# Ordering the first three K/V projection tiles by weight chunk in a fused linear-attention and GLU kernel

## Chip, cores and metric

The kernel runs on one core of a Trainium2 chip. The metric is the device time of one execution in microseconds (us), as the median of several executions. One profiled execution of each kernel shows where the time goes; a profile's span is about 1.7 us shorter than the time of the same execution. The record marks an execution as slow when it lies over 1.5% above the fastest of its kernel. TensorE is called PE (its weight loads PEld), VectorE DVE, ScalarE ACT, GpSimd POOL.

## The reference

The input `x` is 2048 x 1024 in bf16. Only the first part matters here:

```python
qkv = layernorm(x) @ wqkv            # 1024 -> 3 x 1024, 32 heads of 32
phi = lambda t: where(t > 0, t + 1, exp(t)) + 1e-6
kv  = einsum("bhsd,bhse->bhde", phi(k), v)      # summed over all 2048 rows
z   = einsum("bhsd->bhd", phi(k))
o   = (phi(q) @ kv) / (phi(q) . z + 1e-6)
h   = x + o @ wo
# ... then h2 = h + gated MLP(layernorm(h)), well over half of the time
```

## The kernel before

The kernel first makes K and V for 16 row tiles of 128 rows and sums `kv` over them in PSUM, the memory that the matmuls write to. For each tile: layer norm on DVE (with one power on POOL), eight PE transposes (`pt`), a copy to `xnT` on ACT, 16 K matmuls and 16 V matmuls of 128x512 each, and eight small `kv_bank` matmuls. The weights for K and V come in four chunks of 1 MB: two for K (n = 0, 1), two for V.

```python
def ln_transpose(t):
    if t not in x_tiles: load_x(t)              # x tiles: a ring of 3 buffers
    ...                                         # statistics, rstd on POOL, xn on DVE
    for kc in range(KC): nc.tensor.transpose(pt[:, kc, :], xn[...], ident[:])
    nc.scalar.copy(out=xnT[:, :, t * P:(t + 1) * P], in_=pt[:])

def kv_tile(t):
    for n in range(NDC):                        # K: 2 chunks of 8 matmuls
        ...  k_ps += xnT[t] @ wkv_sb[n]
        phi_from_psum(...)                      # exp on ACT, two steps on DVE -> pk_t
    for n in range(NDC):                        # V: 2 chunks of 8 matmuls
        ...  v_ps += xnT[t] @ wkv_sb[NDC + n]
        nc.scalar.copy(out=v_aug[...], in_=v_ps[...])
    for c in range(KC): nc.tensor.matmul(kv_banks[...], lhsT=pk_t[...], rhs=v_aug[...])

for t in range(3): load_x(t)
for i in range(2 * NDC): load_wkv(i)            # 4 x 1 MB, each in 4 DMAs
ln_transpose(0)
for t in range(ST):
    if t + 1 < ST: ln_transpose(t + 1)
    kv_tile(t)
    if t == 1: nc.sync.dma_start(out=wo_sb[:], in_=wo_v)     # 2 MB, needed much later
# ... q projection, attention, MLP
```

A scheduler fixes the order of instructions on each engine when the kernel is built. Each engine then works through its own list in that order, so an instruction that waits holds up all those behind it (in wo_early below, V matmuls whose weights and `xnT` had long been there stood 6.25 us behind tile 3's transposes).

Of the kernel before, what the change touches and what calls it, by code (L numbers as in the profile page):

```python
# [10 lines left out]
FP32 = mybir.dt.float32  # L11
BF16 = mybir.dt.bfloat16
# [9 lines left out]
def kernel(  # L22
# [10 lines left out]
    n_heads: int = N_HEADS,  # L33
    s_half: int = 1024,
    att_banks: int = 2,
):
    nc = tc.nc
    P = nc.NUM_PARTITIONS
# [3 lines left out]
    S, D = x.shape  # L42
    H = n_heads
    Dh = D // H
# [3 lines left out]
    HPC = P // Dh  # L48
    KC = D // P
    ST = S // P  # L50
    FT = F // P
    DW = Dh + 1
# [5 lines left out]
    CW = min(512, D)  # L58
    assert D % CW == 0
    NDC = D // CW  # L60
    CPC = CW // P
# [12 lines left out]
    wo_v = A_wo.rearrange("(kc p) n -> p kc n", p=P)  # L74
# [10 lines left out]
        out=mask[:], in_=mask[:], compare_op=ALU.is_ge, fill=0.0, base=0,  # L85
# [3 lines left out]
        out=mask[:], in_=mask[:], compare_op=ALU.is_ge, fill=0.0, base=Dh - 1,  # L89
# [9 lines left out]
    wo_sb = consts.tile([P, KC, D], BF16)  # L99
# [6 lines left out]
    def ps_tile(shape, dtype, name, tag="bank"):  # L106
        return psum.tile(shape, dtype, tag=tag, name=name, bufs=ps_bufs[tag])

    def layer_norm_stats(pool, src, name):
        fmax = nc.vector.BN_STATS_FMAX  # L110
        nsub = (D + fmax - 1) // fmax
        assert D % nsub == 0
        sub = D // nsub
        st = pool.tile([P, nsub, nc.vector.BN_STATS_DIM], FP32, name=f"{name}_st")
        for i in range(nsub):
            nc.vector.bn_stats(out=st[:, i, :], in_=src[:, i * sub:(i + 1) * sub])  # L116
        mv = pool.tile([P, nc.vector.BN_AGGR_DIM], FP32, name=f"{name}_mv")
        nc.vector.bn_aggr(out=mv[:], in_=st[:])
        rstd = pool.tile([P, 1], FP32, name=f"{name}_rstd")
        nc.vector.tensor_scalar(out=rstd[:], in0=mv[:, 1:2], scalar1=LN_EPS, scalar2=None, op0=ALU.add)  # L120
        nc.gpsimd.tensor_tensor(out=rstd[:], in0=rstd[:], in1=neg_half[:], op=ALU.pow)  # L121
        return mv[:, 0:1], rstd[:, 0:1]

    def phi_from_psum(pool, src_ps, dst, width):
        e = pool.tile([P, width], FP32, name="phi_e")
        nc.scalar.activation(out=e[:], in_=src_ps, func=ACT.Exp)  # L126
        nc.vector.tensor_scalar(out=e[:], in0=e[:], scalar1=PHI_EPS, scalar2=1.0 + PHI_EPS,  # L127
                                op0=ALU.add, op1=ALU.min)
        nc.vector.scalar_tensor_tensor(out=dst, in0=src_ps, scalar=1.0 + PHI_EPS, in1=e[:],
                                       op0=ALU.add, op1=ALU.max)  # L130
# [8 lines left out]
    with ExitStack() as p1:  # L139
        wkvpool = p1.enter_context(tc.tile_pool(name="wkvpool", bufs=2 * NDC))  # L140
        xpool = p1.enter_context(tc.tile_pool(name="xpool", bufs=3))
        pkvpool = p1.enter_context(tc.tile_pool(name="pkvpool", bufs=3))
        small1 = p1.enter_context(tc.tile_pool(name="small1", bufs=4))
        tmp1 = p1.enter_context(tc.tile_pool(name="tmp1", bufs=3))
        wqpool = p1.enter_context(tc.tile_pool(name="wqpool", bufs=NDC))
        big1 = p1.enter_context(tc.tile_pool(name="big1", bufs=1))
        xnT = big1.tile([P, KC, S], BF16)

        assert NKVB <= 2 * att_banks - 1
        kv_banks = []  # L150
        for b in range(NKVB):
            kb = ps_tile([P, KV_PER_BANK, NW], FP32, f"kv_bank{b}", tag=("attA" if b < att_banks else "attB"))
            nc.vector.memset(kb[:], 0.0)
            kv_banks.append(kb)

        wkv_sb = []
        KSPLIT = 4 if KC % 4 == 0 else 1

        def load_wkv(i):
            w_sb = wkvpool.tile([P, KC, CW], BF16, name="wkv_sb")  # L160
            col = D + i * CW
            kg = KC // KSPLIT
            for j in range(KSPLIT):
                nc.sync.dma_start(out=w_sb[:, j * kg:(j + 1) * kg, :], in_=wq_v[:, j * kg:(j + 1) * kg, col:col + CW])
            wkv_sb.append(w_sb)

        x_tiles = {}

        def load_x(t):
            x_sb = xpool.tile([P, D], BF16, name="x_sb")  # L170
            nc.sync.dma_start(out=x_sb[:], in_=x[t * P:(t + 1) * P, :])
            x_tiles[t] = x_sb

        def ln_transpose(t):
            if t not in x_tiles:
                load_x(t)
            x_sb = x_tiles.pop(t)
            mean, rstd = layer_norm_stats(small1, x_sb, "ln1")
            xn = xpool.tile([P, D], BF16, name="xn")
            nc.vector.tensor_scalar(out=xn[:], in0=x_sb[:], scalar1=mean, scalar2=rstd,  # L180
                                    op0=ALU.subtract, op1=ALU.mult)
            pt = ps_tile([P, KC, P], BF16, "pt", tag="bank")
            for kc in range(KC):
                nc.tensor.transpose(pt[:, kc, :], xn[:, kc * P:(kc + 1) * P], ident[:])
            nc.scalar.copy(out=xnT[:, :, t * P:(t + 1) * P], in_=pt[:])  # L185

        def kv_tile(t):
            pk_t = pkvpool.tile([P, D], BF16, name="pk_t")
            for n in range(NDC):
                k_ps = ps_tile([P, CW], FP32, "k_ps")  # L190
                for kc in range(KC):
                    nc.tensor.matmul(k_ps[:], lhsT=xnT[:, kc, t * P:(t + 1) * P], rhs=wkv_sb[n][:, kc, :],  # L192
                                     start=(kc == 0), stop=(kc == KC - 1))
                phi_from_psum(tmp1, k_ps[:], pk_t[:, n * CW:(n + 1) * CW], CW)
            v_aug = pkvpool.tile([P, KC, HPC, DW], BF16, name="v_aug")
            nc.gpsimd.memset(v_aug[:, :, :, Dh:DW], 1.0)
            for n in range(NDC):
                v_ps = ps_tile([P, CW], FP32, "v_ps")
                for kc in range(KC):
                    nc.tensor.matmul(v_ps[:], lhsT=xnT[:, kc, t * P:(t + 1) * P], rhs=wkv_sb[NDC + n][:, kc, :],  # L200
                                     start=(kc == 0), stop=(kc == KC - 1))
                nc.scalar.copy(out=v_aug[:, n * CPC:(n + 1) * CPC, :, 0:Dh],  # L202
                               in_=v_ps[:].rearrange("p (c h e) -> p c h e", c=CPC, h=HPC))
            for c in range(KC):
                b, j = divmod(c, KV_PER_BANK)
                nc.tensor.matmul(kv_banks[b][:, j, :], lhsT=pk_t[:, c * P:(c + 1) * P],  # L206
                                 rhs=v_aug[:, c].rearrange("p h e -> p (h e)"),
                                 start=False, stop=(t == ST - 1), skip_group_check=True)

        for t in range(min(3, ST)):  # L210
            load_x(t)
        for i in range(2 * NDC):
            load_wkv(i)

        ln_transpose(0)
        for t in range(ST):
            if t + 1 < ST:
                ln_transpose(t + 1)
            kv_tile(t)
            if t == 1:  # L220
                nc.sync.dma_start(out=wo_sb[:], in_=wo_v)

        for c in range(KC):
            b, j = divmod(c, KV_PER_BANK)
            nc.vector.tensor_tensor(out=kvaug[:, c], in0=kv_banks[b][:, j, :].rearrange("p (h e) -> p h e", h=HPC),
                                    in1=mask[:], op=ALU.mult)

        wq_sb = []
        for n in range(NDC):
            w_sb = wqpool.tile([P, KC, CW], BF16, name="wq_sb")  # L230
            nc.sync.dma_start(out=w_sb[:], in_=wq_v[:, :, n * CW:(n + 1) * CW])
            wq_sb.append(w_sb)
        prio_before_q = tc.cur_priority
        tc.cur_priority += 100000
        for sc in range(NSC):
            for c in range(KC):
                n, cl = divmod(c, CPC)
                q_ps = ps_tile([P, SC], FP32, "q_ps")
                for kc in range(KC):
                    nc.tensor.matmul(q_ps[:], lhsT=wq_sb[n][:, kc, cl * P:(cl + 1) * P],  # L240
                                     rhs=xnT[:, kc, sc * SC:(sc + 1) * SC],
                                     start=(kc == 0), stop=(kc == KC - 1))
                pq_sb = tmp1.tile([P, SC], BF16, name="pq_sb")
                phi_from_psum(tmp1, q_ps[:], pq_sb[:], SC)
                nc.gpsimd.dma_start(out=pq_dram[sc][c, :, :], in_=pq_sb[:])
        prio_after_q = tc.cur_priority
# [172 lines left out]
```

## Time and profile before

| | before |
|---|---|
| time, median of 4 executions | 872.94 us (872.92 to 873.72) |
| span of the profiled execution | 872.0 us |
| PE busy | 845.0 us, 97% |
| first PE instruction / first K matmul | 8.60 / 10.74 us |
| tile 3's first K matmul | 37.20 us |

The page's busy line of the kernel before reads: busy us of each engine, share of the span, instructions.

```profile
PE 845.0 (97%) x4267; PEld 397.3 (46%) x4352; DVE 350.6 (40%) x715; ACT 191.7 (22%) x273; POOL 42.2 (5%) x92
```

PE is the limit. A change at the start can gain only by starting the chain of PE work earlier or by closing gaps in it. The PE timeline of the kernel before shows them. Columns: start, length (overlapping ends are modelled), engine, line, operation, output<-inputs, count, and in brackets the idle time just ahead and what ended it.

```profile
10.74 5.41 PE L192 MATMUL k_ps<-wkv_sb,xnT 128*128 128x512 bf16 x16 [0.25 <-ACT xnT L185]
...
24.02 3.62 PE L200 MATMUL v_ps<-wkv_sb,xnT 128*128 128x512 bf16 x16
27.48 0.40 PE L206 MATMUL kv_bank<-v_aug,pk_t 128*128 128x132 bf16 x4
28.48 0.29 PE L184 MATMUL pt<-ident,xn 128*128 128x128 bf16 x2 [0.60 <-DVE xn L180]
...
32.62 3.62 PE L200 MATMUL v_ps<-wkv_sb,xnT 128*128 128x512 bf16 x16
36.08 0.40 PE L206 MATMUL kv_bank<-v_aug,pk_t 128*128 128x132 bf16 x4
36.31 0.55 PE L184 MATMUL pt<-ident,xn 128*128 128x128 bf16 x7
36.91 0.40 PE L206 MATMUL kv_bank<-v_aug,pk_t 128*128 128x132 bf16 x4
37.15 0.22 PE L184 MATMUL pt<-ident,xn 128*128 128x128 bf16 x1
37.20 3.62 PE L192 MATMUL k_ps<-wkv_sb,xnT 128*128 128x512 bf16 x15
40.65 3.62 PE L200 MATMUL v_ps<-wkv_sb,xnT 128*128 128x512 bf16 x16
```

The reader is to see three things. The first K matmul is released by the ACT copy, not by a weight. There is one named stop, at 28.48 us: tile 3's transposes wait for the DVE's `xn`. And each turnover, the transposes and `kv_bank` matmuls between the V of one tile and the K of the next, takes 37.20 - 36.08 = 1.12 us.

The first 16 K matmuls take 5.25 us (10.74 to 15.99), later ones 3.45 us. The weight-load timeline of the kernel before (one load per matmul) shows why.

```profile
13.28 0.15 PEld L192 LDWEIGHTS <-xnT 128*128 128x128 bf16 x1 [0.28 <-issue]
13.70 0.15 PEld L192 LDWEIGHTS <-xnT 128*128 128x128 bf16 x1 [0.28 <-issue]
...
14.48 0.10 PEld L192 LDWEIGHTS <-xnT 128*128 128x128 bf16 x1 [0.20 <-issue]
```

The starts are an even 0.427 us apart and then drop to 0.216 us. The even spacing has "issue" and no DMA as what ended the idle time, and it ends where the trace's record has the clock full, at 14.39 us: these matmuls were slow by the clock. The Trainium skill, "TensorE: Matmul & The Clock Gate", "Wait — 56ns, not 53.3ns?", gives 426.7 and 215.7 ns for these two states, and this trace agrees.

The stop at 28.48 us comes from the DVE. Its timeline in the kernel before shows tile 3's statistics behind the first of tile 1's phi steps. The x tile itself was no earlier: its load, queued behind `wo`, landed at 24.25 us, 10.5 us after its issue.

```profile
23.59 0.69 DVE L129 SCALAR_TENSOR_TENSOR pk_t<-k_ps,phi_e 128x512 bf16<-128x512 f32 x1
24.27 0.69 DVE L116 BATCH_NORM_STATS2 ln_st<-x_sb 128x6 f32<-128x512 bf16 x1
...
27.87 0.55 DVE L180 TENSOR_SCALAR xn<-x_sb,ln_mv,ln_rstd 128x1024 bf16<-128x1024 bf16 x1
```

### The profile page before, as it was taken

What the parts mean: (1) busy time and instruction counts of PE and PEld (TensorE: products, weight loads), DVE (VectorE), ACT (ScalarE), POOL (GpSimd) and SP (SyncE); (2) the same over time, 40 slices, a digit from 0 to 9 for tenths busy, and PEclk for the clock granted to TensorE, in tenths of its full rate; (3) what the DMA queues carried; (4) which work ended last, traced back from release to release, by engine and by line L of the source; (5) the groups of instructions that cost most, each with busy time, mean ns of one, the idle gap of its engine ahead of it and who ended that gap; (6) DMA issues with size and microseconds to landing.
All of it is one profiled execution on the core that took longest, in us unless ns stands there. A gap on an engine that the chain in (4) does not pass through costs nothing.

```text
span 872.0 us, 10492 instructions
## 1 busy us (share of the span) xinstructions
PE 845.0 (97%) x4267; PEld 397.3 (46%) x4352; DVE 350.6 (40%) x715; ACT 191.7 (22%) x273; POOL 42.2 (5%) x92
## 2 busy tenths in 40 slices
PE   5999999999999999999999999999999999999998
PEld 3455554444444444444444444444444444444443
DVE  4854324778776414213312411632242142133124
ACT  3344443354534210110011011211101101100110
POOL 2111001211210000000000000000000000000000
PEclk9999999999999999999999999999999999999999
DMA  9710005432352032232232103332311322322002
GB/s 314 240 37 26 0 1 173 135 97 68 97 157 61 13 100 70 85 97 73 85 97 73 56 29 96 121 133 77 93 25 60 97 73 84 97 73 85 1 12 85
DMA packets 73185, 74.09 MB, mean 85 GB/s; under 512 B 18864, under 2 KB 57776, under 8 KB 73136
## 3 DMA queue, kind: packets, MB, share of 16 engines
q1 hardware_dynamic: 71600, 69.21, 25.5%
q0 software_dynamic: 1536, 4.20, 1.4%
q8 instruction: 34, 0.56, 0.3%
q14 instruction: 15, 0.12, 0.0%
HBM read 65.01 MB, written 8.39 MB: 84 GB/s over the span
## 4 chain that ended last, share of the span: by engine, by line
PE 86%; DVE 4%; ACT 3%; issue 2%; DMA 2%; POOL 1%; another core or an unknown queue 0%; SPq 0%; POOLq 0%; ACTq 0%; DVEq 0%
PE u_ps L347 22%; PE g_ps L342 21%; PE d_ps L366 20%; PE k_ps L192 6%; PE v_ps L200 6%; PE wo_ps L284 5%; PE q_ps L240 3%; ACT hn L293 1%; DVE ln_st L116 1%; DVE h_sb L286 1%; ACT v_aug L202 1%; DMA pq_dram<-pq_sb 1%; PE hnT_ps L296 1%; POOL ln_rstd L121 1%; PE kv_bank L206 1%
## 5 line engine op out<-in xcount | busy, mean ns | idle before, releaser
L342 PE MATMUL g_ps<-hnT,wg_sb 128*128 128x512 bf16 x878 | 212.1, 379 | 1.0
L347 PE MATMUL u_ps<-hnT,wu_sb 128*128 128x512 bf16 x878 | 210.8, 379 | 0.8
L352 DVE TENSOR_TENSOR hh<-u_ps,rg 128x512 bf16<-128x512 f32 x112 | 77.3, 690 | 296.2 <-PE u_ps L347 284.9
L366 PE MATMUL d_ps<-wd_sb,hh 128*128 128x512 bf16 x877 | 194.6, 379 | 1.0
L351 ACT ACTIVATE rg<-g_ps 128x512 f32<-128x512 f32 x112 | 66.9, 597 | 460.2 <-PE g_ps L342 454.5
L366 PEld LDWEIGHTS <-hh 128*128 128x128 bf16 x896 | 87.5, 98 | 104.3
L347 PEld LDWEIGHTS <-wu_sb 128*128 128x128 bf16 x896 | 87.3, 98 | 103.4
L342 PEld LDWEIGHTS <-wg_sb 128*128 128x128 bf16 x896 | 87.2, 98 | 102.9
L370 DVE TENSOR_TENSOR h_sb<-d_ps,h_sb 128x512 f32<-128x512 f32 x96 | 66.4, 692 | 78.2 <-PE d_ps L366 77.4
L284 PE MATMUL wo_ps<-wo_sb,oT_sb 128*128 128x512 bf16 x247 | 58.7, 380 | 1.1
L192 PE MATMUL k_ps<-wkv_sb,xnT 128*128 128x512 bf16 x248 | 59.1, 388 | 0.6 <-ACT xnT L185 0.3
L240 PE MATMUL q_ps<-xnT,wq_sb 128*128 128x512 bf16 x249 | 58.8, 379 | 0.2
L200 PE MATMUL v_ps<-wkv_sb,xnT 128*128 128x512 bf16 x250 | 57.5, 379 | 0.4
L127 DVE TENSOR_SCALAR phi_e<-phi_e 128x512 f32<-128x512 f32 x64 | 27.2, 425 | 57.7 <-ACT phi_e L126 57.4
L200 PEld LDWEIGHTS <-xnT 128*128 128x128 bf16 x256 | 25.1, 98 | 30.2
L284 PEld LDWEIGHTS <-oT_sb 128*128 128x128 bf16 x256 | 23.5, 98 | 32.8 <-ACT oT_sb L280 7.8
L192 PEld LDWEIGHTS <-xnT 128*128 128x128 bf16 x256 | 24.7, 99 | 28.1 <-issue 2.4
L121 POOL TENSOR_TENSOR ln_rstd<-ln_rstd,neg_half 128x1 f32<-128x1 f32 x32 | 18.1, 574 | 398.4 <-DVE ln_rstd L120 394.2
L240 PEld LDWEIGHTS <-wq_sb 128*128 128x128 bf16 x256 | 24.0, 98 | 24.0
L286 DVE TENSOR_TENSOR h_sb<-wo_ps,x_sb 128x512 f32<-128x512 f32 x32 | 21.9, 689 | 20.6 <-PE wo_ps L284 18.6
L370 DVE TENSOR_TENSOR o_out<-d_ps,h_sb 128x512 bf16<-128x512 f32 x32 | 21.9, 683 | 19.5 <-PE d_ps L366 18.7
L126 ACT ACTIVATE phi_e<-q_ps 128x512 f32<-128x512 f32 x32 | 19.1, 598 | 36.3 <-PE q_ps L240 32.9
(44 smaller groups left out, 391.5 us busy)
## 6 DMA issues: line engine op xcount, KB each, us to landing
wd_sb<-in_B_W_down_dram SPq DMA_DIRECT2D x8, 1792.0 KB, 8.4
x_sb<-in_A_x_dram SPq DMA_DIRECT2D x32, 256.0 KB, 2.8
wg_sb<-in_B_W_gate_dram SPq DMA_DIRECT2D x8, 1024.0 KB, 5.3
wu_sb<-in_B_W_up_dram SPq DMA_DIRECT2D x8, 1024.0 KB, 7.4
wg_sb<-in_B_W_gate_dram SPq DMA_DIRECT2D x8, 768.0 KB, 4.8
wu_sb<-in_B_W_up_dram SPq DMA_DIRECT2D x8, 768.0 KB, 6.5
wkv_sb<-in_A_wqkv_dram SPq DMA_DIRECT2D x16, 256.0 KB, 5.9
pq_dram<-pq_sb POOLq DMA_DIRECT2D x32, 128.0 KB, 2.4
```

Source lines behind the costliest of these rows:

```text
L127: nc.vector.tensor_scalar(out=e[:], in0=e[:], scalar1=PHI_EPS, scalar2=1.0 + PHI_EPS, op0=ALU.add, op1=ALU.min)
L192: nc.tensor.matmul(k_ps[:], lhsT=xnT[:, kc, t * P:(t + 1) * P], rhs=wkv_sb[n][:, kc, :], start=(kc == 0), stop=(kc == KC - 1))
L200: nc.tensor.matmul(v_ps[:], lhsT=xnT[:, kc, t * P:(t + 1) * P], rhs=wkv_sb[NDC + n][:, kc, :], start=(kc == 0), stop=(kc == KC - 1))
L240: nc.tensor.matmul(q_ps[:], lhsT=wq_sb[n][:, kc, cl * P:(cl + 1) * P], rhs=xnT[:, kc, sc * SC:(sc + 1) * SC], start=(kc == 0), stop=(kc == ...
L284: nc.tensor.matmul(wo_ps[:], lhsT=oT_sb[:, c, :], rhs=wo_sb[:, c, cc * CW:(cc + 1) * CW], start=(c == 0), stop=(c == KC - 1))
L286: nc.vector.tensor_tensor(out=h_sb[:, cc * CW:(cc + 1) * CW], in0=wo_ps[:], in1=x_sb[:, cc * CW:(cc + 1) * CW], op=ALU.add)
L342: nc.tensor.matmul(g_ps[:], lhsT=wg_sb[:, kc, ftl * P:(ftl + 1) * P], rhs=hnT_chunks[sc][:, kc, :], start=(kc == 0), stop=(kc == KC - 1))
L347: nc.tensor.matmul(u_ps[:], lhsT=wu_sb[:, kc, ftl * P:(ftl + 1) * P], rhs=hnT_chunks[sc][:, kc, :], start=(kc == 0), stop=(kc == KC - 1))
L351: nc.scalar.activation(out=rg[:], in_=g_ps[:], func=ACT.Relu)
L352: nc.vector.tensor_tensor(out=hh[:, sc * SC:(sc + 1) * SC], in0=u_ps[:], in1=rg[:], op=ALU.mult)
L366: nc.tensor.matmul(d_ps[:], lhsT=hh_tiles[j][:, stl * P:(stl + 1) * P], rhs=wd_sb[:, j, cc * CW:(cc + 1) * CW], start=(j == 0), stop=(j == ...
L370: nc.vector.tensor_tensor(out=dst[:, cc * CW:(cc + 1) * CW], in0=d_ps[:], in1=h_sb[:, cc * CW:(cc + 1) * CW], op=ALU.add)
```

## The change

Its intent: matmuls that use the first weight chunk can start while the others are still on their way. So the first three tiles all use K chunk 0, then all K chunk 1, and so on; `kv_bank` matmuls come at the end of the group. With it, tile 3's layer norm and transposes move into the middle of the group, and the load of x tile 3 goes out ahead of the 2 MB `wo` load instead of behind it.

```diff
@@ (cut: kv_tile is split into k_part(t, n), v_part(t, n), kv_part(t), bodies unchanged;
@@  pk_t and v_aug get pools of their own, three buffers each as before)
+        G = min(start_group, ST)          # start_group = 3
         ln_transpose(0)
-        for t in range(ST):
+        for n in range(NDC):
+            for t in range(G):
+                if n == 0 and t + 1 < G:
+                    ln_transpose(t + 1)
+                k_part(t, n)
+        if G < ST:
+            ln_transpose(G)
+        for n in range(NDC):
+            for t in range(G):
+                v_part(t, n)
+        for t in range(G):
+            kv_part(t)
+        nc.sync.dma_start(out=wo_sb[:], in_=wo_v)
+        for t in range(G, ST):
             if t + 1 < ST:
                 ln_transpose(t + 1)
             kv_tile(t)
-            if t == 1:
-                nc.sync.dma_start(out=wo_sb[:], in_=wo_v)
```

More of the change, by code (lines that the diff above doesn't have):

```diff
@@ L35 @@
     att_banks: int = 2,
+    start_group: int = 3,
 ):
@@ L141 @@
         xpool = p1.enter_context(tc.tile_pool(name="xpool", bufs=3))
-        pkvpool = p1.enter_context(tc.tile_pool(name="pkvpool", bufs=3))
+        pkvpool = p1.enter_context(tc.tile_pool(name="pkvpool", bufs=max(3, start_group)))
+        pkpool = p1.enter_context(tc.tile_pool(name="pkpool", bufs=max(3, start_group)))
         small1 = p1.enter_context(tc.tile_pool(name="small1", bufs=4))
@@ L185, in ln_transpose @@
             nc.scalar.copy(out=xnT[:, :, t * P:(t + 1) * P], in_=pt[:])
-        def kv_tile(t):
-            pk_t = pkvpool.tile([P, D], BF16, name="pk_t")
-            for n in range(NDC):
-                k_ps = ps_tile([P, CW], FP32, "k_ps")
-                for kc in range(KC):
-                    nc.tensor.matmul(k_ps[:], lhsT=xnT[:, kc, t * P:(t + 1) * P], rhs=wkv_sb[n][:, kc, :],
-                                     start=(kc == 0), stop=(kc == KC - 1))
-                phi_from_psum(tmp1, k_ps[:], pk_t[:, n * CW:(n + 1) * CW], CW)
-            v_aug = pkvpool.tile([P, KC, HPC, DW], BF16, name="v_aug")
-            nc.gpsimd.memset(v_aug[:, :, :, Dh:DW], 1.0)
-            for n in range(NDC):
-                v_ps = ps_tile([P, CW], FP32, "v_ps")
-                for kc in range(KC):
-                    nc.tensor.matmul(v_ps[:], lhsT=xnT[:, kc, t * P:(t + 1) * P], rhs=wkv_sb[NDC + n][:, kc, :],
-                                     start=(kc == 0), stop=(kc == KC - 1))
-                nc.scalar.copy(out=v_aug[:, n * CPC:(n + 1) * CPC, :, 0:Dh],
-                               in_=v_ps[:].rearrange("p (c h e) -> p c h e", c=CPC, h=HPC))
+        pk_tiles = {}
@@ new lines, with k_part @@
+        vaug_tiles = {}
+        def k_part(t, n):
+            if t not in pk_tiles:
+                pk_tiles[t] = pkpool.tile([P, D], BF16, name="pk_t")
+            pk_t = pk_tiles[t]
+            k_ps = ps_tile([P, CW], FP32, "k_ps")
+            for kc in range(KC):
+                nc.tensor.matmul(k_ps[:], lhsT=xnT[:, kc, t * P:(t + 1) * P], rhs=wkv_sb[n][:, kc, :],
+                                 start=(kc == 0), stop=(kc == KC - 1))
+            phi_from_psum(tmp1, k_ps[:], pk_t[:, n * CW:(n + 1) * CW], CW)
@@ new lines, in v_part @@
+        def v_part(t, n):
+            if t not in vaug_tiles:
+                v_aug = pkvpool.tile([P, KC, HPC, DW], BF16, name="v_aug")
+                nc.gpsimd.memset(v_aug[:, :, :, Dh:DW], 1.0)
+                vaug_tiles[t] = v_aug
+            v_aug = vaug_tiles[t]
+            v_ps = ps_tile([P, CW], FP32, "v_ps")
+            for kc in range(KC):
+                nc.tensor.matmul(v_ps[:], lhsT=xnT[:, kc, t * P:(t + 1) * P], rhs=wkv_sb[NDC + n][:, kc, :],
+                                 start=(kc == 0), stop=(kc == KC - 1))
+            nc.scalar.copy(out=v_aug[:, n * CPC:(n + 1) * CPC, :, 0:Dh],
+                           in_=v_ps[:].rearrange("p (c h e) -> p c h e", c=CPC, h=HPC))
@@ L204, in kv_tile, with kv_part @@
+        def kv_part(t):
+            pk_t = pk_tiles.pop(t)
+            v_aug = vaug_tiles.pop(t)
             for c in range(KC):
@@ L208, in kv_tile @@
                                  start=False, stop=(t == ST - 1), skip_group_check=True)
+        def kv_tile(t):
+            for n in range(NDC):
[3 more added lines that the diff above has]
+            kv_part(t)
         for t in range(min(3, ST)):
@@ L213 @@
             load_wkv(i)
+        G = min(start_group, ST)
         ln_transpose(0)
-        for t in range(ST):
+        for n in range(NDC):
+            for t in range(G):
+                if n == 0 and t + 1 < G:
+                    ln_transpose(t + 1)
+                k_part(t, n)
+        if G < ST:
+            ln_transpose(G)
+        for n in range(NDC):
+            for t in range(G):
+                v_part(t, n)
+        for t in range(G):
+            kv_part(t)
+        nc.sync.dma_start(out=wo_sb[:], in_=wo_v)
+        for t in range(G, ST):
             if t + 1 < ST:
```

## The prediction

> **What bounds the kernel now.** The page's busy table: TensorE (PE) is busy 845.0 of 872.0 us (97%); in the chain of waits PE holds 86%. The only large gap is the start: in the PE timeline the first instruction is at 8.60 us (x load, layer norm), the first K matmul at 10.74 us. From there to 140 us PE is nearly gapless.
>
> **Does the start wait for weights, as the change assumes?** No. The first K matmul's releaser is the ACT copy of xnT (0.25 us). The first eight K matmuls are slow (weight loads start 0.43 us apart until 14.1 us, 0.216 us afterwards), but evenly so: the cold clock. The Trainium skill, "TensorE: Matmul & The Clock Gate", "Wait — 56ns, not 53.3ns?", states 426.7 ns at N=512 cold and 215.7 ns warm, which agrees. So the 1.7 us lost there is not DMA. The weight chunks (16 DMAs issued from 2.2 to 12.5 us, median 5.9 us to landing) arrive just ahead of use: tile 0 runs from 14.1 to 19.6 us at full rate, and the waits view lists no PE wait on a weight DMA.
>
> **What the change moves.** The same 96 projection matmuls, 24 transposes and 24 kv matmuls, the same memory; after tile 3 the PE's instruction order is unchanged. New order: two tiles' transposes, 8 K, 8 transposes, 40 K, 8 transposes, 48 V, 24 kv, 8 transposes, then as before. The load of x tile 3 now goes ahead of the 2 MB wo load.
>
> **On the critical path.**
> - Before has one stall: layer norm of tile 3 is late (x tile 3 queued behind wo), PE idle 0.60 us at 28.5 us, released by DVE xn. V starts at 24.02, 32.62, 40.65: 8.60 against the steady 8.03. The earlier x load and the longer K run remove it: -0.57 us.
> - Each steady turnover loses 0.14 us: 8.03 against 32 x 0.216 + 8 x 0.060 + 8 x 0.064 = 7.90 (the last four kv matmuls wait for the 0.60 us ACT copy of v_aug). At the group's end the first 16 kv matmuls take 0.95 us and cover that copy: three turnovers, up to -0.42 us.
> - Extra switches between transposes and K: estimate +0.1 us.
> - New waits I looked for: K needs one PSUM bank per 1.73 us, and ACT 0.60 + DVE 1.12 us per bank keep up. DVE blocks on x tile 3 until about 19 us (estimate: issue 12.9 + 5.9), within four banks' slack.
>
> Sum: -0.9 us of 872.94, about 0.1%. PE is critical to the end, so it should survive as a rigid shift: 872.0 us, range 871.3 to 872.9. Chances: faster by 2% 0.01, within 2% 0.98, slower by 2% 0.01.
>
> **What would show each step.** First K matmul still near 10.74 us, first eight still 0.43 us apart, no weight-DMA wait in either kernel; the idle at 28.5 us gone; tile 3's K at about 36.4 us instead of 37.37; later PE pieces earlier by 0.9 us; PE busy time nearly unchanged.
>
> **What would make it wrong.** The cold clock ending at another moment (part of its 1.7 us either way). The DVE, now placed to normalise tiles 4 to 9 before tile 3's phi, blocking on x loads behind 4 MB of wo and wq, so that K finds no free bank (1 to 3 us lost). The attention stage absorbing the shift in a DMA wait (0.89 us at 162.6 us).

## The result

| | before | after |
|---|---|---|
| time, median | 872.94 us (872.26 to 873.72, 15 runs) | 871.57 us (871.11 to 874.64, 10 runs) |
| ratio | | 0.9987, 95% interval 0.9978 to 0.9996 |
| span of the profiled execution | 872.0 us | 870.2 us |
| first K matmul | 10.74 us | 10.57 us |
| tile 3's first K matmul | 37.20 us | 35.41 us |

A ratio is the mean time of one kernel's fast runs over that of the other's of the same rounds, so it is not quite the ratio of the medians. The medians differ by 1.37 us. The profiles differ more, 1.8 us, partly because the profiled execution of before was the slowest of its 15 (873.72 us).

The page's busy line of the kernel after, and its PE timeline to the point where tile 3 begins:

```profile
PE 844.1 (97%) x4267; PEld 397.3 (46%) x4352; DVE 350.4 (40%) x715; ACT 191.4 (22%) x273; POOL 42.2 (5%) x92
```

```profile
10.56 3.28 PE L198 MATMUL k_ps<-wkv_sb,xnT 128*128 128x512 bf16 x8 [0.25 <-ACT xnT L187]
13.68 0.61 PE L186 MATMUL pt<-ident,xn 128*128 128x128 bf16 x8
14.13 8.80 PE L198 MATMUL k_ps<-wkv_sb,xnT 128*128 128x512 bf16 x39
22.76 0.61 PE L186 MATMUL pt<-ident,xn 128*128 128x128 bf16 x8
23.21 10.52 PE L210 MATMUL v_ps<-wkv_sb,xnT 128*128 128x512 bf16 x47
33.57 1.56 PE L220 MATMUL kv_bank<-v_aug,pk_t 128*128 128x132 bf16 x24
34.97 0.61 PE L186 MATMUL pt<-ident,xn 128*128 128x128 bf16 x8
35.41 0.81 PE L198 MATMUL k_ps<-wkv_sb,xnT 128*128 128x512 bf16 x2
```

(A count of 39 or 47 is one record missing from the trace; the times show 40 and 48.) The first K matmul is no earlier for the change: it waits for the same ACT copy, and the 0.17 us come before it, from the x load and layer norm. The stop at 28.48 us is gone, and the three turnovers have become one.

From first K to tile 3's K it took 26.46 us before and 24.84 us after, 1.62 us less. The clock explains part: in this execution it was full at 13.39 us, in the profile of before at 14.39 us (the trace's record of the granted clock). I take the cold clock's cost as what the first K matmuls take over their 3.45 us for 16 (or 1.73 us for 8) at the full rate: 1.80 us before, 1.38 us after. What is left for the order of work is 1.62 - 0.42 = 1.20 us.

### The profile page after: what moved, and what is told of

Its sections match the earlier page's. It is cut to its first block, busy times and chain, and to the rows that moved or that the text cites. A ratio compares the mean times of both kernels' runs of the same rounds, so it can differ in the third digit from the quotient of the medians.

```text
span 870.2 us, 10491 instructions
## 1 busy us (share of the span) xinstructions
PE 844.1 (97%) x4267; PEld 397.3 (46%) x4352; DVE 350.4 (40%) x715; ACT 191.4 (22%) x273; POOL 42.2 (5%) x92
## 4 chain that ended last, share of the span: by engine, by line
PE 86%; DVE 4%; ACT 3%; DMA 2%; issue 2%; POOL 1%; another core or an unknown queue 0%; POOLq 0%; ACTq 0%; DVEq 0%; SPq 0%
PE u_ps L380 21%; PE g_ps L375 21%; PE d_ps L399 20%; PE k_ps L198 6%; PE v_ps L210 6%; PE wo_ps L317 4%; PE q_ps L273 3%; DMA pq_dram<-pq_sb 2%; DVE ln_st L117 1%; ACT hn L326 1%; DVE h_sb L319 1%; PE hnT_ps L329 1%; PE kv_bank L220 1%; POOL ln_rstd L122 1%; ACT v_aug L212 1%
```

## The experiments

All 12 runs computed the right result. Each was timed in five rounds beside the kernel before. One table holds them; "net" is the time from first K to tile 3's K without the cold clock's cost as just defined (no correction where dummy matmuls warm the clock).

| kernel | time, median | before in the same batch | ratio (95% interval) | clock full at | first K | tile 3's K | net |
|---|---|---|---|---|---|---|---|
| (before, profile) | | | | 14.39 | 10.74 | 37.20 | 24.66 |
| (after, profile) | | | | 13.39 | 10.57 | 35.41 | 23.46 |
| after_again | 872.33 | 873.06 | 0.9992 (0.9979 to 1.0004) | 11.86 | 10.58 | 35.53 | 24.33 |
| x3_first | 874.05 | 873.06 | 1.0007 (0.9995 to 1.0020) | 14.58 | 10.35 | 36.54 | 24.10 |
| kv_deferred | 872.14 | 873.06 | 0.9991 (0.9978 to 1.0003) | 13.57 | 10.61 | 35.53 | 23.46 |
| wo_early | 879.30 | 873.06 | 1.0078 (1.0064 to 1.0091) | 12.11 | 10.60 | 43.19 | 31.85 |
| warm_after | 872.24 | 873.38 | 0.9986 (0.9974 to 0.9998) | 4.84 | 10.04 | 34.87 | 24.83 |
| warm_t3_late | 871.96 | 873.38 | 0.9988 (0.9976 to 1.0000) | 4.98 | 10.54 | 34.07 | 23.53 |
| warm_ungrouped | 872.21 | 873.38 | 0.9989 (0.9976 to 1.0001) | 5.76 | 10.01 | 35.27 | 25.26 |
| t3_late | 872.02 | 873.38 | 0.9985 (0.9973 to 0.9996) | 14.05 | 10.52 | 35.72 | 23.54 |
| warm_x6 | 874.70 | 873.30 | 1.0021 (1.0002 to 1.0040) | 4.82 | 9.84 | 33.31 | 23.47 |
| warm_ungrouped_x6 | 872.50 | 873.30 | 0.9994 (0.9982 to 1.0006) | 7.01 | 10.11 | 34.91 | 24.80 |
| pipe_x6 | 869.19 | 873.30 | 0.9957 (0.9944 to 0.9970) | 13.03 | 10.49 | 35.20 | 23.47 |
| best | 869.00 | 873.30 | 0.9951 (0.9939 to 0.9963) | 4.73 | 10.07 | 33.54 | 23.47 |

The intervals of single kernels are as wide as the effect of the change, so the traces decide most questions here.

### after_again: the changed kernel repeated

No edit. 

> The changed kernel unaltered, as the yardstick of this batch. Expected about 1.2 us under the kernel before: 1.21 us from the turnovers of the first three tiles (3.95 us of transposes, kv matmuls and stalls before, 2.74 us after, both summed from the PE start times of the two traces). What is left of the difference of the two profiles (0.41 us of cold clock, 0.17 us of start) should not repeat, if it is chance: the number of cold K matmuls in this profile should vary between 7 and 9.

The gain was 0.73 us by the medians, short of the expected 1.2, and its interval includes none. The number of cold K matmuls varied more than expected: here the clock was full at 11.86 us and only three or four of them were slow, against seven to nine. Yet tile 3 began no earlier. The PE and DVE timelines of after_again:

```profile
13.38 8.80 PE L198 MATMUL k_ps<-wkv_sb,xnT 128*128 128x512 bf16 x40
22.73 0.62 PE L186 MATMUL pt<-ident,xn 128*128 128x128 bf16 x8 [0.56 <-DVE xn L182]
```

```profile
18.96 1.29 DVE L117 BATCH_NORM_STATS2 ln_st<-x_sb 128x6 f32<-128x512 bf16 x2 [1.87 <-DMA x_sb<-in_A_x_dram]
...
22.13 0.55 DVE L182 TENSOR_SCALAR xn<-x_sb,ln_mv,ln_rstd 128x1024 bf16<-128x1024 bf16 x1 [0.44 <-POOL ln_rstd L122]
```

A new wait shows: PE asks for tile 3's transposes in the middle of the group, but x tile 3 comes in behind all 4 MB of weights, at 18.96 us, and its layer norm ends at about 22.7 us. A clock that is full earlier only meets that wait earlier. I had not predicted this. A smaller stop follows at 43.54 us: 0.32 us, for the DVE.

### x3_first: the x load alone

```diff
-            if t == 1:
+            if t == 2:
                 nc.sync.dma_start(out=wo_sb[:], in_=wo_v)
```

> The kernel before with one thing of the change alone: the load of x tile 3 goes out ahead of the wo load. My theory (the stall at tile 3's layer norm is a late x load): the idle of 0.60 us at 28.5 us is gone, 0.4 to 0.7 us faster than before, V starts 8.03 us apart from tile 1 on. Rival A (the gain comes from grouping by weight chunk): no gain, 0.0 us. Rival B (the stall is the crowded DVE, not the load): the idle stays.

In the trace the theory held. Net time fell by 0.56 us (24.66 to 24.10), against 0.57 us in my prediction, and V matmuls start 8.03 us apart from tile 1 on. The PE timeline of x3_first has no stop at tile 3's transposes:

```profile
27.61 0.55 PE L184 MATMUL pt<-ident,xn 128*128 128x128 bf16 x7
28.21 0.40 PE L206 MATMUL kv_bank<-v_aug,pk_t 128*128 128x132 bf16 x4
```

The edit moves two things at once: with the earlier load the scheduler also placed tile 3's statistics ahead of tile 1's phi on DVE (at 19.15 us instead of 24.27 us). So the load and the DVE's order are not told apart by this run. The landing times tell part: x tile 3 landed at 19.12 us, and its statistics began at 19.15; in the kernel before it landed at 24.25 us, so no order of DVE could have begun them before that. Once begun, they and tile 3's `xn` took 2.9 us here and 4.2 us before, where other steps stood between. In the time the expectation failed: the median was 1 us slower. Two of its five runs took 872.07 and 872.65 us, three took 874.05 to 874.71 us. The profiled execution (874.34 us) is of the second kind, and the table by stretch shows what it lost. Columns: stretch and length, busy us of PE, PEld, DVE, ACT, POOL, granted clock, DMA share, GB/s.

```profile
253.50:256.90 3.40, 1.30 (x12) 0.85 (x13) 1.51 (x3) 1.88 (x2) 0.47 (x1) 1.00 0.18 66
256.90:260.40 3.50, 3.50 (x14) 1.70 (x13) 1.54 (x5) 0.40 (x2) 0.00 (x0) 0.51 0.00 0
```

In the attention stage PE was busy for only 1.30 of 3.40 us, and for the next 3.41 us the clock was granted at half, about 1.7 us lost. The kernels before and after show no such stretch in their profiles. So about 2 us that come and go between executions of one kernel lie far from the edit, and the edit's half microsecond can't be read from the times. That this accounts for all three slow runs is not shown: only one of them was profiled, and one of the others lists a mean clock of 1.0.

### kv_deferred: the change without its grouping by weight chunk

```diff
-        for n in range(NDC):
-            for t in range(G):
-                if n == 0 and t + 1 < G:
-                    ln_transpose(t + 1)
-                k_part(t, n)
-        if G < ST:
-            ln_transpose(G)
-        for n in range(NDC):
-            for t in range(G):
-                v_part(t, n)
+        for t in range(G):
+            if t + 1 < ST:
+                ln_transpose(t + 1)
+            for n in range(NDC):
+                k_part(t, n)
+            for n in range(NDC):
+                v_part(t, n)
```

> The changed kernel with the grouping by weight chunk taken out: the first three tiles run K and V each in turn (weight chunks used in the old order), only the kv matmuls stay at the end of the group and the x load of tile 3 ahead of wo. My theory (no weight was ever waited for): the same gain as the changed kernel within 0.3 us, about 1.2 us under before. Rival A (earlier matmuls because of weight grouping): the gain is lost, within 0.3 us of before, and PE waits for weights at 14 to 19 us.

This is the central test. The PE timeline of kv_deferred:

```profile
10.61 5.07 PE L198 MATMUL k_ps<-wkv_sb,xnT 128*128 128x512 bf16 x16 [0.25 <-ACT xnT L187]
15.52 3.62 PE L210 MATMUL v_ps<-wkv_sb,xnT 128*128 128x512 bf16 x16
...
33.68 1.57 PE L220 MATMUL kv_bank<-v_aug,pk_t 128*128 128x132 bf16 x24
```

It has the weights in the old order, yet its net time is 23.46 us, the same as that of the changed kernel, and its time (872.14 us) equals that of after_again (872.33 us) within the spread. No wait for a weight appears. With the clock cold, the grouping by weight chunk shows no worth; the whole gain comes with the x load and the deferred `kv_bank` matmuls. The step from x3_first to kv_deferred, 24.10 - 23.46 = 0.64 us, is the worth of the deferral (with the pools of their own that it needs).

### wo_early: the change with the wo load put back ahead of x tile 3

```diff
         ln_transpose(0)
+        nc.sync.dma_start(out=wo_sb[:], in_=wo_v)
 ...
-        nc.sync.dma_start(out=wo_sb[:], in_=wo_v)
```

> The changed kernel with the wo load put back ahead of the x load of tile 3. If the x load is what matters, tile 3's x lands about 5 to 6 us later (2 MB at about 370 GB/s), at about 24.5 us, its layer norm ends at about 27 us, and the PE, which wants tile 3's transposes at 22.8 us, stops for 3 to 5 us: 2 to 4 us slower than before. If the longer K run alone gives enough slack (as my prediction said beside the load), no stop and the same time as the changed kernel.

It took 6.2 us longer than before, more than I expected. The PE timeline of wo_early and its table by stretch (columns as above):

```profile
28.56 1.03 PE L186 MATMUL pt<-ident,xn 128*128 128x128 bf16 x8 [6.25 <-DVE xn L182]
```

```profile
22.30:28.60 6.30, 0.05 (x2) 0.04 (x2) 4.97 (x13) 0.60 (x1) 0.55 (x1) 0.78 1.08 362
28.60:33.10 4.50, 4.50 (x18) 2.16 (x19) 2.23 (x8) 1.21 (x2) 1.09 (x2) 0.56 0.90 255
```

PE stopped 6.25 us, and the clock went to half for 6.83 us, of which 4.0 us (28.56 to 32.59) fell on matmuls: the 48 V matmuls took 11.95 us instead of 10.36. So the earlier x load is no extra: in the grouped order it is needed. The longer K run alone gives no slack, contrary to the reasoning in my prediction, which had named the two side by side: the new order asks for tile 3's transposes at 22.1 us, the old one not before 27.7 us.

### warm_after: the changed kernel with a warm clock

```diff
+    wu_src = consts.tile([P, 512], BF16)
+    nc.vector.memset(wu_src[:], 0.0)
 ...
+        warm_ps = ps_tile([P, CW], FP32, "warm_ps")
+        for _ in range(18):
+            nc.tensor.matmul(warm_ps[:], lhsT=wu_src[:, 0:P], rhs=wu_src[:], start=True, stop=True)
```

> The changed kernel with 18 dummy matmuls on the PE from about 1.6 us on, so that its clock is at full rate before the first transposes. New theory, from the repeat of the changed kernel (clock full at 11.86 us instead of 13.39 us, yet tile 3's K no earlier): in the changed order the PE asks for tile 3's transposes in the middle, and these can't start before 22.7 us, because x tile 3 lands behind all 4 MB of weights at 18.96 us. Then a warm clock gains nothing: first K matmul at about 10.1 us at 0.216 us each, then a stop of 1.5 to 2.5 us ahead of tile 3's transposes, these at 22.7 us as before, tile 3's K at 35.5 us; time within 0.4 us of the changed kernel (about 1 us under before). Rival (only the clock counts): tile 3's K 2 us earlier than 35.5 us, time 3 us under before.

The clock was full at 4.84 us and the first eight K matmuls took 1.73 us instead of 3.11. The PE timeline of warm_after shows where that went:

```profile
22.21 0.62 PE L192 MATMUL pt<-ident,xn 128*128 128x128 bf16 x8 [1.19 <-DVE xn L188]
```

PE stopped there and tile 3's K began at 34.87 us. Counted from start to start, the run of 40 K matmuls and the stop took 9.99 us instead of 8.63, so the stop is 1.36 us. The time was 1.1 us under before, as for the changed kernel. The theory held, though the stop was under the expected 1.5 to 2.5 us and tile 3's K came 0.6 us earlier than expected: in the changed order this wait pins the start of tile 3 once the clock is full early.

### warm_t3_late: the same with tile 3's transposes behind the V matmuls

```diff
-        if G < ST:
-            ln_transpose(G)
         for n in range(NDC):
             for t in range(G):
                 v_part(t, n)
+        if G < ST:
+            ln_transpose(G)
```

> As warm_after, and tile 3's transposes moved behind the 48 V matmuls. By the new theory the stop goes: 48 K and 48 V matmuls back to back from about 10.1 us, tile 3's K at about 33.2 us, 2.3 us earlier than in the changed kernel; time 2.5 to 3.5 us under before. If weights hold the grouped order too (last V chunk lands at 18.0 us, first needed at about 20.5 us), there would be a PE stop at the first V matmuls; I expect none.

The stop went, the net time was 23.53 us without any correction, and no V matmul waited for a weight. Tile 3's K came at 34.07 us rather than 33.2 us, in part because layer norm ended 0.5 us later in this execution than in warm_after. But the time was only 1.4 us under before, short of the expected 2.5 to 3.5. The PE timeline of warm_t3_late has the reason:

```profile
42.80 0.41 PE L226 MATMUL kv_bank<-v_aug,pk_t 128*128 128x132 bf16 x4 [1.03 <-DVE pk_t L132]
```

Tile 3's `kv_bank` matmuls wait for `pk_t`, which comes late from DVE: the gain turned into a new wait.

### warm_ungrouped: no grouping, warm clock

Edit: kv_deferred plus the dummy matmuls. 

> kv_deferred (K and V of each tile in turn, no grouping by weight chunk) with the warm clock. Now the old order would use the last V chunk of tile 0 at 15.3 to 16.7 us, but it lands at about 18.0 us: I expect the PE to stop for weights by about 1.4 us within tile 0's K and V matmuls, tile 3's K at about 34.5 us, time about 1.3 us slower than warm_t3_late. That would be the worth of grouping by weight chunk once the clock is warm. Rival (weights never matter): same as warm_t3_late within 0.3 us, no stop in tile 0.

Here the weights are waited for. The PE timeline of warm_ungrouped:

```profile
13.48 2.08 PE L216 MATMUL v_ps<-wkv_sb,xnT 128*128 128x512 bf16 x8
15.72 1.34 PE L216 MATMUL v_ps<-wkv_sb,xnT 128*128 128x512 bf16 x4 [0.17 <-DMA wkv_sb<-in_A_wqkv_dram]
17.23 0.59 PE L216 MATMUL v_ps<-wkv_sb,xnT 128*128 128x512 bf16 x2 [0.17 <-DMA wkv_sb<-in_A_wqkv_dram]
17.98 0.59 PE L216 MATMUL v_ps<-wkv_sb,xnT 128*128 128x512 bf16 x2 [0.16 <-DMA wkv_sb<-in_A_wqkv_dram]
```

The 16 V matmuls of tile 0 took 4.93 us instead of 3.45, so 1.48 us were lost to weights, close to the expected 1.4 us. The bracketed idle times are smaller because modelled ends overlap the gaps; start to start tells the truth. Before tile 3, then, the grouping does what it was meant to do, once the clock is not cold. Tile 3's K came at 35.27 us, later than the expected 34.5: the last `kv_bank` matmuls of the group waited another 0.3 us for DVE's `pk_t`. In the time (872.21 against 871.96 us) the difference is not clear of noise. In the two traces 0.67 us of the 1.20 us at tile 3's K are left at the last V matmul (138.34 against 137.67 us), after waits such as the one of 1.03 us in warm_t3_late.

### t3_late: tile 3's transposes late, cold clock

Edit: as in warm_t3_late, without the dummy matmuls. 

> The changed kernel with only tile 3's transposes moved behind the V matmuls, clock left cold. In runs where the clock is full late (13.4 us) there was no stop to remove, so no gain; where it is full early (11.9 us), 0.7 us gained. On average 0 to 0.6 us under the changed kernel, that is 1.0 to 1.9 us under before; no PE idle ahead of tile 3's transposes in its profile.

It came out 1.36 us under before by the medians, with no stop in its profile and the tightest spread of all (871.73 to 872.09 us). Against the changed kernel this is no clear gain: the clock in its profile was full late, at 14.05 us, where I expected none.

### warm_x6 and warm_ungrouped_x6: six buffers for x

```diff
-            x_sb = xpool.tile([P, D], BF16, name="x_sb")
+            x_sb = xpool.tile([P, D], BF16, name="x_sb", bufs=6)
```

The first is warm_t3_late with this edit: 

> warm_t3_late with six buffers instead of three for the x tiles. Reading of warm_t3_late: its gain at tile 3's K (34.07 us) was given back at 41.5 us, where PE stops 1.25 us for DVE's pk_t, DVE having sat 2.7 us in front of late x tiles, whose loads wait for one of three buffers. With six buffers that stop goes: first K to tile 3's K 23.5 us (34.0 us on the clock of the trace), no PE stop over 0.3 us between 10 and 60 us, time 2.3 to 3.5 us under before. If the stop stays or moves, the x loads are held by the transfers ahead of them, not by the buffers, and the time stays at 1.0 to 1.5 us under before.

The second is warm_ungrouped with it: 

> The same without the grouping by weight chunk (as warm_ungrouped, which stopped 1.5 us in five V matmuls of tile 0). With the later stops gone, the difference to warm_x6 is the worth of grouping under a warm clock: 1.3 to 1.5 us from first K to tile 3's K (25.0 us against 23.5 us), and 1.0 to 1.7 us in time. Rival: no difference in time, because a later wait takes it back.

Up to tile 3's K both went as expected: net 23.47 against 24.80 us, so grouping is worth 1.33 us under a warm clock. The record of tile 3's first K matmul is missing in the trace of warm_ungrouped_x6. Its PE timeline shows 15 of 16, the first 0.66 us behind the start of eight transposes that take 0.45 us; I take 35.12 - 0.216 = 34.91 us.

```profile
34.46 0.61 PE L192 MATMUL pt<-ident,xn 128*128 128x128 bf16 x8
35.12 3.40 PE L204 MATMUL k_ps<-wkv_sb,xnT 128*128 128x512 bf16 x15
```

What followed did not go as expected. The PE timeline of warm_x6:

```profile
41.03 0.41 PE L226 MATMUL kv_bank<-v_aug,pk_t 128*128 128x132 bf16 x4 [0.65 <-DVE pk_t L132]
...
43.90 0.41 PE L226 MATMUL kv_bank<-v_aug,pk_t 128*128 128x132 bf16 x4 [2.07 <-DVE pk_t L132]
```

The stops grew, so my reading of warm_t3_late (too few x buffers alone) falls. In this trace DVE was at work without a wait for x from 28 to 38.4 us: with more x tiles in reach, the scheduler put the layer norms of more later tiles ahead of tile 3's phi, in a list that DVE works off in order (the statistics of eight tiles were finished between 25 us and that phi, against six in the changed kernel). Tile 3's first phi step on DVE began at 39.37 us, against 37.99 us in the changed kernel, though its K matmuls began 2.1 us earlier. Between the two halves of that phi DVE then does wait for an x tile, 0.65 us at 41.63 us. A fixed order with phi first was not tried, so this last step rests on the trace alone. In three of its six runs warm_x6 also shows a mean clock of 0.995 to 0.996 and 876.2 to 877.9 us; its three runs at a clock of 1.0 took 872.7 to 873.2 us, about what warm_ungrouped_x6 took.

### pipe_x6 and best: kv matmuls behind the next tile's K

pipe_x6 is t3_late with six x buffers and, in the later tiles:

```diff
-            kv_tile(t)
+            for n in range(NDC):
+                k_part(t, n)
+            if t > G:
+                kv_part(t - 1)
+            for n in range(NDC):
+                v_part(t, n)
+        kv_part(ST - 1)
```

> t3_late with six x buffers, cold clock as in the kernel before, and in tiles 3 to 15 the kv matmuls of each tile issued behind the next tile's K matmuls, so that none waits for the ACT copy of v_aug. My figure for a turnover is 1.12 us before against 0.91 us without the wait; 12 turnovers would give 2.4 us: time 3.3 to 4.4 us under before. If the turnover's loss is something else (switching between forms of matmul), the gain stays at that of t3_late, 1.0 to 1.5 us under before.

It gained 4.1 us over before, in the expected range. The PE timeline of pipe_x6:

```profile
42.55 3.62 PE L198 MATMUL k_ps<-wkv_sb,xnT 128*128 128x512 bf16 x15
46.00 0.63 PE L220 MATMUL kv_bank<-v_aug,pk_t 128*128 128x132 bf16 x8
...
50.37 3.62 PE L198 MATMUL k_ps<-wkv_sb,xnT 128*128 128x512 bf16 x15
```

A tile now takes 50.37 - 42.55 = 7.82 us; in the kernel before it took 40.65 - 32.62 = 8.03 us (V start to V start). The 0.21 us are the wait for ACT's copy of `v_aug`. In the kernel before they lie at one place: the seventh transpose starts at 36.64 us and the `kv_bank` matmul behind it at 36.91, 0.27 us later instead of 0.056. The ACT timeline of the kernel before has the second half of the copy ending just ahead of that:

```profile
36.28 0.59 ACT L202 CAST v_aug<-v_ps 128x512 bf16<-128x512 f32 x1 [1.14 <-PE v_ps L200]
```

Over 12 later turnovers that is an estimated 2.5 us. From tile 3's first K to the last V matmul, 102.60 us pass before and in t3_late, 100.09 us in pipe_x6: 2.51 us less. The gains over before of pipe_x6 and t3_late, from two batches, differ by 4.11 - 1.36 = 2.75 us. Six buffers with a cold clock were not run alone; t3_late has no named PE stop in this stretch that they could remove.

best has all edits together: 

> All together: grouping, tile 3's transposes late, six x buffers, kv matmuls behind the next K, warm clock. If the gains add up, 4.5 to 6 us under before, about 868 us, within 2% but clear of noise; the group and the clock gain about 3 us, the turnovers 2.4 us.

It took 869.0 us, 4.3 us under before, slightly short of the expectation. The warm clock brought tile 3 forward by 1.7 us against pipe_x6, but the medians differ by only 0.2 us. In its trace PE stops about 0.9 us for DVE's `pk_t` at 40 us, and again for 0.4 us at 43.5 us, as in warm_x6, though less. It is half a per cent under the kernel before and, across batches, about 0.4% under the changed one.

## Why the prediction was right

- **Size.** 872.0 us was predicted, with 871.3 to 872.9 as range; 871.57 us was measured, and 872.33 us in a second batch. That the figure fell between the two medians is in part luck: the order's effects were put 0.3 us too low (below), and a wait that I missed takes 0.87 us of them back where the clock is full early (net 24.33 us in after_again against 23.46).
- **"Does the start wait for weights, as the change assumes?" "No."** In the words of an expectation, "no weight was ever waited for". Shown by kv_deferred, which has the weights in the old order and the same gain. It is true of the cold clock only. With a warm clock the old order loses 1.33 to 1.48 us to weights (warm_ungrouped_x6, warm_ungrouped) and the grouped order nothing.
- **The stop at tile 3's layer norm, -0.57 us:** x3_first measured -0.56 us in the trace. That the longer K run helps was wrong: without the earlier load, wo_early stopped 6.25 us.
- **Turnovers, -0.42 us:** measured -0.64 us (x3_first to kv_deferred), 0.21 us each instead of 0.14. The term was too small mainly because I priced a transpose at 0.064 us; in the traces eight take 0.45 us, 0.056 us each. pipe_x6 found the same 0.21 us in the later tiles.
- **Extra switches, +0.1 us:** nothing. The net times of the changed kernel and of kv_deferred, with different numbers of switches in the K run, are both 23.46 us.
- **The sum** of the order's effects is then -1.20 us against the predicted -0.9 us. It explains the profile; the time adds the moment at which the clock is full, which differs from run to run.
- **The clock**, named as a risk, was one: it was full anywhere from 11.86 to 14.58 us in kernels without dummy matmuls. But an early clock did not help the changed kernel, since x tile 3 then holds PE (after_again, warm_after). This wait is the step that I missed: I had looked at its effect on phi and PSUM banks, where no PE stop shows up to tile 3, and not at the transposes themselves: PE can ask for them from 22.0 us on (after_again), and they can start at 22.7 us.
- **Rigid shift.** Tile 3's K was 1.79 us earlier, the span at the end 1.8 us shorter: in this pair of traces the attention stage took nothing back. (The 37.37 us in the prediction is a misreading; the trace of before has 37.20 us.)

## What to carry to other kernels

Ahead of reordering work for data that "comes late", look for the wait: here the matmuls that started evenly at half the rate were slow by the clock, and no DMA was waited for. A tile whose load is queued behind a large transfer can pin the order whatever else is made faster, so place its consumer by when it can be ready; and as each engine works off a fixed list, more prefetch can put later tiles' work ahead of what the PE needs now (read from the trace of warm_x6, not tested apart). A small wait in a turnover that repeats 12 times was worth more here than everything at the start.

## What the Trainium skill lacked or had wrong

- "TensorE: Matmul & The Clock Gate", "What you observe", puts the change of clock at around 4 us of activity, ±500 ns from run to run. Here it came 3.4 us (after_again: 8.44 to 11.86 us) to 6.4 us (x3_first: 8.21 to 14.58 us) after the first PE instruction, where PE begins with 16 transposes and a short gap, and 3.5 us (best: 1.26 to 4.73 us) to 5.75 us (warm_ungrouped_x6: 1.26 to 7.01 us) where it begins with dummy matmuls back to back. The spread is wider than ±500 ns. The page's own later remark, that one kernel measured 6, 11 or 14 cold matmuls by the phase of a free-running window, is nearer to it.
- The same page, "Why this matters for your kernels", advises against PE-idle gaps of more than about 3 us. In x3_first the longest idle ahead of a drop was 2.54 us: PE was busy 1.30 of 3.40 us, and the clock was then granted at half for 3.41 us. In the changed kernel the same place had an idle of 1.57 us and kept its clock.
- The same page, "Part 4: PE-mode transpose", says that the full clock does not engage for matmuls in transpose mode and gives 275 to 390 ns for one of 128x128. The PE transposes here, matmuls against an identity, follow the clock like other matmuls: 0.107 us from start to start in the cold state (kernel before, 8.68 to 10.18 us), 0.056 us in the warm one (eight in 0.45 us in the kernel after). The trace does not say whether they use that mode, so the page is not shown to be wrong. What it lacks is their spacing: its figures are the time of one transpose, which this trace puts at 0.22 us in the warm state, with a modelled end.
